# Moving the two x buffers from the end of each SBUF partition to the place ahead of the weights

## The chip, the cores and the metric

The kernel runs on one core of a Trainium2 chip. The metric is the device time of one execution in microseconds (us); three runs of the kernel before gave 540.85, 543.45 and 539.7, so the median is 540.85 us.

## What is computed

A linear-attention pass (4 sequences, 8 heads, 768 tokens, 48 channels per head) whose output feeds a gated feed-forward layer over 3,072 tokens. Its weights come as 64-bit floats, its other inputs as 32-bit floats. Cut to what matters:

```python
for t in range(S):                                   # attention, per batch and head
    cur = einsum('bhd,bhe->bhde', u[None] * k[:, :, t], v[:, :, t])
    y[:, :, t] = einsum('bhd,bhde->bhe', r[:, :, t], state + cur)
    state = w[None, :, :, None] * state + einsum('bhd,bhe->bhde', k[:, :, t], v[:, :, t])
x = y.transpose(0, 2, 1, 3).reshape(3072, 384)
gate = 1 / (1 + exp(-(x @ w_gate)))                   # 384 -> 1536
out = (gate * (x @ w_val)) @ w_out                    # 1536 -> 384
```

## The kernel before

Tokens go in 12 chunks of 64 per sequence. Two chunks of all four sequences make one tile `xt[ti]` of 512 token columns, so there are 6 tiles (`TILES`). The attention of a chunk runs in two groups of heads; each group's output is copied from PSUM into the tile's `xt` by ScalarE (`x_high`, L456, the part that the matmul format keeps) and VectorE (`x_low`, L460, the rest), and small DMAs of the SP queue (`fill`) put the rows of the last two heads into their places. Every tile lies in one of two buffers of 16,384 bytes in each of the 128 partitions, taken in turn.

The feed-forward layer takes a tile's 512 columns through 12 slices f of 128 hidden channels. `up(f)` (L502) issues 18 matmuls: for gate and value each, three slices kt of the 384 channels by three passes (low weights by high x, high by high, high by low), all 9 adding up in one PSUM bank of the ring of three. The moving operand (the one that streams through the array) is `xt[:, kt, b, cols]`, the stationary one a 128 by 128 block of `wx`. Every matmul is preceded by its own weight load. Then come sigmoid (L511, ScalarE), product (L515, VectorE), and the split of the result into `h` high (L520, ScalarE) and low (L524, GpSimd). `down(f)` (L540) issues 9 matmuls whose moving operand is `h` and whose stationary operand is the third part of the same `wx`, into three accumulators. It goes pass by pass over the three output parts; at f = 11 it goes part by part, three passes in a row into the same accumulator. In the last tile the third part is split into two halves of 256 columns, so that there `down` has 12 matmuls.

The order of the work is written out by hand: `START` for the first tile, where weights are also loaded and converted (columns there go in halves of 256 for f = 0 and 1), then the loop over the items of tiles 1 to 5, which sets the pieces of attention (lines L320, L348 and L403, matmuls of at most 64 columns) between `up` and the `down` of the slice before. `tc.manual_schedule` keeps that order on PE, SP, DVE, ACT and POOL; only places in memory and the waits are worked out by the program. So a `down(f-1)` stands on PE's queue right behind `up(f)` or behind a piece of attention.

Places come from the pools in the order in which they are opened. Behind the constants lie `wp` (12 weight buffers of 9,216 bytes), `hp` (`sg`), `hq` (`h`), `wtmp` (`wf`), `ach` (`chan`), `atk` (`toks`), `adk` (`dec`) and `xp` (`xt`). At the end, a conditional block recomputes everything in another way if a decay is out of range; with these inputs it isn't entered.

Of the kernel before, what the change touches and what calls it, by code (L numbers as in the profile page):

```python
# [9 lines left out]
F32 = mybir.dt.float32  # L10
F32R = mybir.dt.float32r
# [8 lines left out]
P = 128  # L20
# [4 lines left out]
CT = B * C  # L25
# [32 lines left out]
def rwkv_then_moe(ctx: ExitStack, tc: tile.TileContext, wd, ch, tk, rt, ut, wt, rk0, vn0, wd0, out):  # L58
    nc = tc.nc

    const = ctx.enter_context(tc.tile_pool(name="const", bufs=1))
    wp = ctx.enter_context(tc.tile_pool(name="wp", bufs=1))
    hp = ctx.enter_context(tc.tile_pool(name="hp", bufs=2))
    hq = ctx.enter_context(tc.tile_pool(name="hq", bufs=2))
# [4 lines left out]
    main = ctx.enter_context(ExitStack())  # L69
    ach = main.enter_context(tc.tile_pool(name="ach", bufs=3))  # L70
    atk = main.enter_context(tc.tile_pool(name="atk", bufs=3))
    adk = main.enter_context(tc.tile_pool(name="adk", bufs=2))
    xp = main.enter_context(tc.tile_pool(name="xp", bufs=2))


    def two_banks():
# [179 lines left out]
    xt, dec, ga, yb, kv = {}, {}, {}, {}, {}  # L256
# [180 lines left out]
    def x_of(n, k):  # L437
        c, g = GROUPS[n]
        ti = TILE_OF[c]
        if ti not in xt:  # L440

            xt[ti] = xp.tile([P, 4, 2, 512], F32R, name="xt")
        co = CT * TILES[ti].index(c)
        return [
            (
                xt[ti][lo:hi, 2 * g : 2 * g + 2, k, co + 128 * be : co + 128 * be + 128],
                yb[n][be][lo:hi, 0:256].rearrange("q (p x) -> q p x", p=2),
            )

            for be in range(2)  # L450
            for lo, hi in (((0, 48), (64, 112)) if ti == 0 and g == 0 else ((0, 112),))
        ]

    def x_high(n):
        for x, y in x_of(n, 0):
            nc.scalar.copy(out=x, in_=y)  # L456

    def x_low(n):
        for (x, y), (hi, _) in zip(x_of(n, 1), x_of(n, 0)):
            nc.vector.tensor_tensor(x, y, hi, ALU.subtract)  # L460
# [164 lines left out]
    for step in START.split():  # L625
        name, _, arg = step.partition(".")
# [22 lines left out]
    for i in range(n0, len(items)):  # L649
        ti, h, f = items[i]  # L650
# [44 lines left out]
    with tc.If(bad != 0):  # L695
        with ExitStack() as g:
            gp = g.enter_context(tc.tile_pool(name="gp", bufs=1))
# [21 lines left out]
            with tc.For_i(0, NC) as c:  # L719
# [38 lines left out]
                    out=xg[bass.ds(c, 1)].rearrange("o q p t -> (o q) p t"),  # L758
                    in_=yc.rearrange("q p b i -> q p (b i)"),
                )  # L760
            xr = gp.tile([P, 3, 2, CT], F32, name="xr")
            x = gp.tile([P, 3, 2, 512], F32R, name="xgr")
            with tc.For_i(0, NC, 2) as c:
                for j in range(3):
                    for to, lo, n, p in (
# [113 lines left out]
```

## Time and profile before

| what | value |
|---|---|
| median of three runs | 540.85 us (539.7 to 543.45) |
| profiled execution: first to last instruction | 538.6 us |
| what lies around that span, against the median | 540.85 - 538.6 = 2.25 us |
| mean granted TensorE clock | 0.996 |
| PE busy | 519.2 us, 96% of the span |
| DVE, ACT, POOL busy | 218.3, 171.8 and 175.0 us |

For the profiled execution the profile gives the span alone; its own time with what lies around it was not taken apart from the three runs. PE is TensorE's matmuls, PEld its weight loads, DVE the vector engine, ACT the scalar engine, POOL GpSimd. A matmul's duration runs from its issue to its modelled end, so it is longer than the step from one matmul to the next: steps are taken from the starts of a row of matmuls.

### The profile page before, as it was taken

How to read it: one execution, taken by the hardware profiler on the slowest of the kernel's cores; microseconds unless marked ns; L12 is line 12 of the kernel's file. 1: busy time of each engine (PE TensorE's matmuls, PEld its weight loads, DVE VectorE, ACT ScalarE, POOL GpSimd, SP SyncE). 2: the span in 40 equal slices, each digit the busy share in tenths (PEclk: the TensorE clock that was granted, in tenths of full speed). 3: DMA queues.
4: the chain of work that ended last, by engine and by line, in shares of the span. 5: the costliest groups of instructions: out<-in, count | busy, mean ns of one | idle time of the engine just before them, and what ended most of it. 6: DMA issues, size and time to landing. Idle time of an engine off the chain costs nothing.

```text
span 538.6 us, 12067 instructions
## 1 busy us (share of the span) xinstructions
PE 519.2 (96%) x5268; PEld 426.9 (79%) x5268; DVE 218.3 (41%) x379; ACT 171.8 (32%) x358; POOL 175.0 (32%) x156
## 2 busy tenths in 40 slices
PE   4879999999999999999999999999999999999996
PEld 3769878788788887888888888888888887888885
DVE  7798999942343342432423414313414311111111
ACT  5576654522132232231332222222322212221121
POOL 3353330002814444234145144144242311111120
PEclk9999999999999999999999999999999999999999
DMA  8886903053022213220303402203300001100001
GB/s 324 314 301 239 382 2 99 16 204 128 2 86 86 70 48 141 85 84 3 95 3 104 145 7 79 67 28 106 144 1 16 12 1 19 60 0 1 0 1 63
DMA packets 15707, 48.03 MB, mean 89 GB/s; under 512 B 2369, under 2 KB 5057, under 8 KB 14241
## 3 DMA queue, kind: packets, MB, share of 16 engines
q1 hardware_dynamic: 15360, 46.81, 25.2%
q8 instruction: 43, 0.70, 0.5%
q10 hardware_dynamic: 288, 0.39, 0.2%
q14 instruction: 16, 0.12, 0.1%
HBM read 40.12 MB, written 4.72 MB: 83 GB/s over the span
## 4 chain that ended last, share of the span: by engine, by line
PE 91%; DVE 4%; DMA 3%; ACT 1%; issue 0%; SPq 0%; DVEq 0%; ACTq 0%
PE ring L502 55%; PE acc L540 27%; PE ring L320 5%; PE sc L348 2%; DMA toks<-in_tk 1%; DMA chan<-in_ch 1%; PE sc L403 1%; DMA wr<-in_wt 1%; DVE score L362 1%; PE sc L540 1%; DVE wf L243 1%; DVE wf L244 1%; DVE wx L253 0%; ACT wf L236 0%; DVE wf L242 0%
## 5 line engine op out<-in xcount | busy, mean ns | idle before, releaser
L502 PE MATMUL ring<-xt,wx 128*128 128x512 f32 (+1 forms) x1332 | 317.1, 392 | 2.1 <-ACT wx L250 1.7
L502 PEld LDWEIGHTS ring<-xt,wx 128*128 128x128 f32 x1332 | 247.4, 191 | 57.5 <-ACT wx L250 1.9
L524 POOL TENSOR_TENSOR h<-sg,h 128x512 fp32r<-128x512 f32 (+1 forms) x68 | 91.8, 1350 | 332.4 <-ACT h L520 326.5
L540 PE MATMUL acc<-h,wx 128*128 128x512 f32 (+1 forms) x666 | 160.9, 383 | 0.0
L515 DVE TENSOR_TENSOR sg<-ring,sg 128x512 f32<-128x512 f32 (+1 forms) x74 | 50.0, 676 | 272.7 <-PE ring L502 272.7
L540 PEld LDWEIGHTS acc<-h,wx 128*128 128x128 f32 x666 | 119.6, 188 | 24.3
L511 ACT ACTIVATE sg<-ring 128x512 f32<-128x512 f32 (+1 forms) x74 | 43.4, 586 | 181.2 <-PE ring L502 181.2
L520 ACT CAST h<-sg 128x512 fp32r<-128x512 f32 (+1 forms) x74 | 45.3, 612 | 109.0 <-DVE sg L515 109.0
L422 ACT ACTIVATE state<-state,every 112x96 f32<-112x96 f32 x80 | 23.5, 363 | 26.7 <-PE ring L320 26.7
L460 DVE TENSOR_TENSOR xt<-ring,xt 112x256 fp32r<-112x256 f32 (+1 forms) x52 | 19.9, 418 | 26.9 <-ACT xt L456 26.9
L301 POOL TENSOR_TENSOR dec<-chan,every 128x512 f32<-128x512 f32 x20 | 23.8, 1190 | 13.8 <-PE ring L320 5.9
L362 DVE COPY_PREDICATED score<-masks,sc 128x512 f32<-128x512 int32 x32 | 23.8, 743 | 0.9
L456 ACT CAST xt<-ring 112x256 fp32r<-112x256 f32 (+1 forms) x52 | 17.1, 372 | 17.2 <-PE ring L320 15.6
L320 PE MATMUL ring<-score,toks 64*64 64x64 f32 (+1 forms) x768 | 18.6, 230 | 4.0 <-DVE score L362 2.0
L311 POOL TENSOR_TENSOR toks<-toks,tabn 128x384 f32<-128x384 f32 x18 | 19.7, 1093 | 0.0
L320 PEld LDWEIGHTS ring<-score,toks 64*48 64x48 f32 (+1 forms) x768 | 15.3, 133 | 5.2 <-POOL dec L301 1.9
L250 ACT CAST wx<-wf 128x1152 fp32r<-128x1152 f32 (+1 forms) x13 | 14.1, 1084 | 15.1 <-DVE wf L244 15.1
L244 DVE SCALAR_TENSOR_TENSOR wf<-wr,wf 128x1152 int32<-128x1152 int32 (+1 forms) x13 | 18.4, 1415 | 0.5
L320 PEld LDWEIGHTS ring<-dec,state 48*48 48x48 f32 (+1 forms) x704 | 12.0, 127 | 7.4 <-issue 6.7
L348 PE MATMUL sc<-dec,chan 48*64 48x64 f32 x768 | 17.6, 231 | 0.1
L289 POOL TENSOR_TENSOR dec<-dec,toks 128x384 f32<-128x384 f32 x16 | 16.3, 1016 | 1.2
L243 DVE SCALAR_TENSOR_TENSOR wf<-wr,wf 128x1152 int32<-128x1152 int32 (+1 forms) x13 | 16.5, 1266 | 0.5
(62 smaller groups left out, 253.0 us busy)
## 6 DMA issues: line engine op xcount, KB each, us to landing
wr<-in_wt SPq DMA_DIRECT2D x11, 1152.0 KB, 8.7
chan<-in_ch SPq DMA_DIRECT2D x24, 512.0 KB, 4.5
toks<-in_tk SPq DMA_DIRECT2D x24, 400.0 KB, 4.9
out_y<-wf SPq DMA_DIRECT2D x16, 256.0 KB, 2.3
dec<-in_rt SPq DMA_DIRECT2D x16, 192.0 KB, 2.6
xt<-xt SPq DMA_DIRECT2D x30, 64.0 KB, 2.3
wr<-in_wt SPq DMA_DIRECT2D x2, 576.0 KB, 5.2
xt<-xt SPq DMA_DIRECT2D x12, 32.0 KB, 4.9
```

What stands on the lines that cost most here:

```text
L244: nc.vector.scalar_tensor_tensor(g, low, 29, g, ALU.logical_shift_right, ALU.bitwise_or)
L301: eng.tensor_tensor(v4(t[:, 0]), v4(chan[n][:, 0]), bc2(table_of(n)), ALU.mult)
L320: nc.tensor.matmul(yb[n][bank][64 * half : 64 * half + m, cs], lhsT, rhs, start=first, stop=stop, skip_group_check=True,)
L348: nc.tensor.matmul(sc[64 * gm : 64 * gm + 64, be ^ gm, o : o + C], kk[row, cs : cs + C], rr[row, cs : cs + C], start=True, stop=True,)
L362: nc.vector.copy_predicated(t.rearrange("q (b m i) -> q b m i", b=2, m=4), masks[:, m].bitcast(I32).unsqueeze(1).unsqueeze(1).broadcast_to ...
L422: nc.scalar.activation(st[:, p, s], st[:, p, s], AF.Copy, scale=pw[0:112, 4 * g + 2 * p + s, 64:65],)
L502: nc.tensor.matmul(o[:, self.cols], w[a][:, g * DM + kt * P : g * DM + (kt + 1) * P], self.x[:, kt, b, self.cols], start=(k == 0), stop=(k ...
L511: nc.scalar.activation(sg[:, c], self.pair[f][0][:, c], AF.Sigmoid)
L515: nc.vector.tensor_tensor(sg[:, c], self.pair.pop(f)[1][:, c], sg[:, c], ALU.mult)
L520: nc.scalar.copy(out=h[:, 0, c], in_=sg[:, c])
L524: eng.tensor_tensor(h[:, 1, c], self.sg.pop(f)[:, c], h[:, 0, c], ALU.subtract)
L540: nc.tensor.matmul(acc[:, to], w[a][:, 2 * DM + d * P : 2 * DM + (d + 1) * P], h[:, b, cols], start=(f == 0 and k == 0 and self.cols.start ...
```

## The change

`xp` is opened right behind the constants, ahead of the weights, and stays open to the end; its tile gets the tag `xt`. The conditional block takes its two x tiles from `xp` under the same tag, since the room that they had lies elsewhere now.

```diff
     const = ctx.enter_context(tc.tile_pool(name="const", bufs=1))
+    xp = ctx.enter_context(tc.tile_pool(name="xp", bufs=2))
     wp = ctx.enter_context(tc.tile_pool(name="wp", bufs=1))
...
     adk = main.enter_context(tc.tile_pool(name="adk", bufs=2))
-    xp = main.enter_context(tc.tile_pool(name="xp", bufs=2))
...
-            xt[ti] = xp.tile([P, 4, 2, 512], F32R, name="xt")
+            xt[ti] = xp.tile([P, 4, 2, 512], F32R, name="xt", tag="xt")
...
-            xr = gp.tile([P, 3, 2, CT], F32, name="xr")
-            x = gp.tile([P, 3, 2, 512], F32R, name="xgr")
+            xr = xp.tile([P, 3, 2, CT], F32, name="xr", tag="xt")
+            x = xp.tile([P, 3, 2, 512], F32R, name="xgr", tag="xt")
```

In bytes from the end of the constants, worked out from the shapes of the tiles (r is the remainder of the offset by 512):

| tile | before | r | after | r |
|---|---|---|---|---|
| `xt`, two of 16,384 | 162,176 | 384 | 0 | 0 |
| `wx`, twelve of 9,216 | 0 | 0 | 32,768 | 0 |
| `sg`, two of 2,048 | 110,592 | 0 | 143,360 | 0 |
| `h`, two of 4,096 | 114,688 | 0 | 147,456 | 0 |
| `wf`, two of 4,608 | 122,880 | 0 | 155,648 | 0 |
| `chan`, three of 4,096 | 132,096 | 0 | 164,864 | 0 |
| `toks`, three of 3,200 | 144,384 | 0, 128, 256 | 177,152 | 0, 128, 256 |
| `dec`, two of 4,096 | 153,984 | 384 | 186,752 | 384 |

Both versions end at 194,944. A block that a weight load reads starts a multiple of 512 bytes into `wx`, and a 512-column slice of `xt` or `h` a multiple of 2,048 into its tile.

## Rows read from the trace of the kernel before

**Rows 1.** The page, part 1: busy time, share of the span, instructions.

```profile
PE 519.2 (96%) x5268; PEld 426.9 (79%) x5268; DVE 218.3 (41%) x379; ACT 171.8 (32%) x358; POOL 175.0 (32%) x156
```

**Rows 2.** The page, part 4: the chain that ended last, shares by line.

```profile
PE ring L502 55%; PE acc L540 27%; PE ring L320 5%; PE sc L348 2%; DMA toks<-in_tk 1%; DMA chan<-in_ch 1%; PE sc L403 1%; DMA wr<-in_wt 1%; DVE score L362 1%; PE sc L540 1%; DVE wf L243 1%; DVE wf L244 1%; DVE wx L253 0%; ACT wf L236 0%; DVE wf L242 0%
```

**Rows 3.** Stretches: length, busy us (count) per engine, granted clock, DMA share, GB/s.

```profile
57.77:83.03 25.26, 24.97 (x317) 20.32 (x316) 23.99 (x30) 14.52 (x24) 9.57 (x5) 1.00 0.34 139
83.03:466.50 383.47, 383.17 (x3577) 311.07 (x3576) 135.43 (x251) 106.31 (x222) 129.45 (x112) 1.00 0.22 68
466.50:538.60 72.10, 67.16 (x325) 55.81 (x323) 9.41 (x14) 13.76 (x23) 12.92 (x10) 0.99 0.03 12
```

**Rows 4.** Waits of PE's matmuls, 83 to 466 us: total us, times, longest.

```profile
PE ring L320 <- issue: 0.2, 1, 0.2
```

**Rows 5.** Groups by line and shape: busy us, mean ns | idle before.

```profile
L502 PE MATMUL ring<-xt,wx 128*128 128x512 f32 x1260 | 304.6, 395 | 0.0
...
L540 PE MATMUL acc<-h,wx 128*128 128x512 f32 x594 | 152.6, 395 | 0.0
...
L502 PE MATMUL ring<-xt,wx 128*128 128x256 f32 x72 | 12.5, 343 | 2.1 <-ACT wx L250 1.7 <-DVE wx L253 0.5
```

**Rows 6.** Timeline of PE from 460.1 us: start, length, work.

```profile
460.26 2.22 PE L540 MATMUL acc<-h,wx 128*128 128x512 f32 x9
462.31 4.36 PE L502 MATMUL ring<-xt,wx 128*128 128x512 f32 x18
466.50 0.74 PE L540 MATMUL acc<-h,wx 128*128 128x512 f32 x3
```

**Rows 7.** Groups of PE, 462.6 to 466.3 us.

```profile
L502 PE MATMUL ring<-xt,wx 128*128 128x512 f32 x18 | 4.4, 395 | 0.0
```

**Rows 8.** Timeline of PE, 101.05 to 103.6 us, within a double `down`.

```profile
100.70 3.11 PE L540 MATMUL acc<-h,wx 128*128 128x512 f32 x13
```

**Rows 9.** Groups of PE in the same stretch.

```profile
L540 PE MATMUL acc<-h,wx 128*128 128x512 f32 x13 | 3.1, 389 | 0.0
```

**Rows 10.** Timeline of PE, 48.8 to 50.0 us: `h` at 256 columns.

```profile
48.60 1.60 PE L540 MATMUL acc<-h,wx 128*128 128x256 f32 x12
```

**Rows 11.** Groups of PE in that stretch.

```profile
L540 PE MATMUL acc<-h,wx 128*128 128x256 f32 x12 | 1.6, 283 | 0.0
```

**Rows 12.** Timeline of PE, 31.4 to 32.9 us: x at 256 columns.

```profile
31.14 1.95 PE L502 MATMUL ring<-xt,wx 128*128 128x256 f32 x15
```

**Rows 13.** Groups of PE in that stretch.

```profile
L502 PE MATMUL ring<-xt,wx 128*128 128x256 f32 x15 | 1.9, 282 | 0.0
```

**Rows 14.** Timeline of all engines from 455.5 us.

```profile
455.70 1.30 POOL L524 TENSOR_TENSOR h<-sg,h 128x512 fp32r<-128x512 f32 x1 [5.38 <-ACT h L520]
...
461.78 0.58 ACT L554 COPY wf<-acc 128x512 f32<-128x512 f32 x1
...
461.95 1.30 POOL L524 TENSOR_TENSOR h<-sg,h 128x512 fp32r<-128x512 f32 x1 [4.95 <-ACT h L520]
```

**Rows 15.** The chain in order of time, last tile: start, us, what.

```profile
519.00 4.18 PE ring L502 x18
```

**Rows 16.** Groups by line and shape: writers of `xt` and of `wf`.

```profile
L460 DVE TENSOR_TENSOR xt<-ring,xt 112x256 fp32r<-112x256 f32 x44 | 16.6, 417 | 24.3 <-ACT xt L456 24.3
...
L456 ACT CAST xt<-ring 112x256 fp32r<-112x256 f32 x44 | 14.2, 373 | 16.5 <-PE ring L320 15.0 <-DVE state L433 1.5
...
L557 DVE COPY wf<-acc 128x256 f32<-128x256 f32 x5 | 2.1, 424 | 2.0 <-ACT wf L556 2.0
L556 ACT COPY wf<-acc 128x256 f32<-128x256 f32 x5 | 1.9, 373 | 0.8 <-PE acc L540 0.8
```

**Rows 17.** The page, part 6: DMA issues, KB each, us to landing.

```profile
xt<-xt SPq DMA_DIRECT2D x30, 64.0 KB, 2.3
```

**Rows 18.** Timeline, 292 to 304 us: a piece of attention.

```profile
299.89 0.68 PE L320 MATMUL ring<-dec,state 48*64 48x64 f32 x32
...
300.39 0.65 PE L348 MATMUL sc<-dec,chan 48*64 48x64 f32 x32
```

## The prediction

> **What bounds the kernel now.** I read the page's busy times first: PE is busy 96% of the span, no other engine over 41% [rows 1]. The chain of waits names the kind of PE work: 55% of the span is L502 (moving operand x), 27% L540 (moving operand h) [rows 2]. The stretches say where this holds: from 57.77 us on PE is busy all but 0.3 us of each stretch up to 466.5, at a granted clock of 1.00, the 2.4 GHz level [rows 3], and its matmuls wait 0.2 us in 383 [rows 4]. So from about 57 us to the end the time is the number of matmuls by the step from one to the next, and only what changes a step can change the time. No instruction, count or order changes here; places in memory alone do.
>
> So the question is whether the step depends on where an operand lies. The trace holds a comparison. Behind a run of x matmuls the next run of h starts at 466.50, the x run itself at 462.31 [rows 6]; 18 x matmuls last 4.36 us to the last end, one lasts 0.395 [rows 7], so a step is (4.36 - 0.395) / 17 = **233.2 ns**. In a long run of h, once it has settled, 13 last 3.11 and one lasts 0.389 [rows 8, 9]: (3.11 - 0.389) / 12 = **226.8 ns**. The two have the same 128 rows, 512 columns, format and clock, and a weight load ahead of each. There are 1,260 of the first kind and 594 of the second [rows 5].
>
> What else could tell them apart? An x run adds up 9 matmuls in one PSUM bank and uses the same weights twice in three steps, an h run changes bank and weights at each step. But at f = 11 `down` does both: three passes in a row into one accumulator, weights in the order of `up`. The run at 460.26 is such a one, since the copy of the accumulator into `wf` follows at 461.78 [rows 14]; it takes 462.31 - 460.26 = 2.05 us for 9 [rows 6], 227.8 a step with the first two still settling. Neither bank nor weight order slows it. What remains is the moving operand's tile. By the table of offsets x starts at remainder 384 by 512, and weights and h at 0; and x lies in the last 32,768 bytes that the program uses. Which of the two counts the trace can't say, as nothing else wide is read from there; the change alters both. After it x starts 114,688 + 32,768 = 147,456 bytes ahead of h, nine times 16,384, so every remainder by powers of two up to 16,384 is the same for x as for h.
>
> **The change part by part.**
>
> *L502 at 512 columns.* I let x take h's step: 233.2 - 226.8 = 6.4 ns. An `up` has 18: 0.115 us. There are 70 such `up`: 10 in tile 0, 48 in tiles 1 to 4, 12 in the last. The settling of h behind x goes too, 9 x (227.8 - 226.8) = 0.009 us. So 58 slices save 0.124 us each, 7.2 us. In the last tile an x run takes 4.18 on the chain [rows 15], 232.2 a step, so 18 x 5.4 = 0.097, by 12: 1.2 us; its `down` mixes 512 and 256 columns and I give it nothing. Sum **8.3 us**. The bounds: nothing at the one end, as no row shows an operand read from both places. At the other, the whole cost per matmul beyond its columns vanishes: h takes (1.60 - 0.283) / 11 = 119.7 ns at 256 columns [rows 10, 11], so 256 columns cost 107.1, 512 cost 214.2, and 1,260 x (233.2 - 214.2) = 23.9 us. The other sign is priced among the rivals. I take 8.3, since the nearest row is h, whose remainders x gets.
>
> Back-to-back weight loads and matmuls are the subject of the Trainium skill, TensorE: Matmul & The Clock Gate, Part 2 (Step-by-step: what each phase is for): PE has two independent read ports on SBUF, so that the next weights take no bandwidth from the running matmul. By that rule no place could collide with another, and the sum would be 0 us instead of 8.3; it is the first rival below.
>
> *L502 at 256 columns.* 72 of them [rows 5]. At 31.14 us 15 last 1.95 and one 0.282 [rows 12, 13], 119.1 a step, against h's 119.7. If x takes h's step it loses 72 x 0.6 = 0.04 us, and in that stretch PE waits for weights anyway: 0. This row also speaks against my reading: at 256 columns x pays nothing for its place. It says that the cost isn't one per matmul; a meeting of two streams at some point of the longer read would look so.
>
> *Writers of x.* ScalarE writes 112 x 256 to x in 373 ns and the same width to `wf`, which lies elsewhere, in 373; VectorE takes 417 and 424, though the first also reads x [rows 16]. Place costs them nothing: 0. If it did, PE covers it, as DVE and ACT are busy 135 and 106 of 383 us [rows 3].
>
> *DMAs.* The copies within x, 30 of 64 KB at 2.3 us [rows 17], keep partitions, sizes and their turn on SP's queue: 0; PE covers a slip as long as a tile's last fill lands before its first `up`. No step is moved past another on any queue, and no wait is added outside the conditional block.
>
> *Everything else* moves up by 32,768 bytes with its remainders unchanged: 0. Attention's operands get the place that x had; that is the slower rival.
>
> *Would a faster PE meet a wait?* The low half of h is ready at 455.70 + 1.30 = 457.00, and its `down` starts at 460.26 [rows 6, 14]: 3.3 us to spare, against 0.12 us that a slice loses. PE stays the bound, and the saving passes through.
>
> The sum is made on the profiled span: 538.6 - 8.3 = 530.3. The median of the runs stands 2.25 above that span, so 540.85 - 8.3 = **532.5 us**.
>
> **The rivals.**
>
> *Place is nothing (same).* The 6.4 ns belong to something of L502 that stays, such as the ring's banks or the length of its runs. For it: at 256 columns there is no difference [rows 10 to 13]. Against it: the f = 11 run shares its order and its bank use with x and steps at 227.8 [rows 6]. Time: 540.85 us. The rule of the two ports gives the same 540.85; the trace doesn't bear it out so far, as its two kinds of steps differ by 6.4 ns in spite of equal sizes, but it shows no collision as such either. I put half of this rival's chance on it.
>
> *Part of it.* The remainder matters, but x's step and h's lock in only some runs, as the unsettled first steps behind each change of line suggest. Half the gain, 4.2 us, is 536.7, within 1%.
>
> *The end of the partition costs, and attention inherits it (slower).* If what lies in the last 32,768 bytes is read more slowly by PE, x leaves and `dec` with parts of `chan` and `toks` arrive. The page counts 5,268 matmuls [rows 1]; `up` has 1,332, `down` 74 x 9 + 12 x 3 = 702, so about 3,200 small ones are left. If each paid 6.4 ns in full, that is 20.5, and less the 8.3 the kernel would take 553 us. It decides from (8.3 + 5.4) / 3,200 = 4.3 ns each, which makes it 1% slower. Against it: 32 of them start in 300.39 - 299.89 = 0.50 us, 15.6 ns apart [rows 18], several in the array at once, so that a price per matmul would be shared (by four: 5.1 us, a net gain of 3); and x's 256-column reads from that place paid nothing.
>
> *It doesn't do what it says.* The places are worked out from shapes; if the pools were laid out in another order, x would keep its place: 540.85, part of the first rival.
>
> **How the numbers follow.** Forecast (x takes h's step, gain 6 to 10 us, 531 to 535): 0.62. More, towards 214 ns a step: 0.04. Place is nothing: 0.18, on half of it the rule. Part: 0.08. Slower: 0.08. A measurement of this kernel tells about 1% (5.4 us) from no change. So faster by over 1%: 0.66, within: 0.26, slower: 0.08. The range reaches from 530, just under the forecast's own 531 to 535, over the part and the unchanged case to 541.5; it leaves out the slower case, the large gain, and the upper part of the spread of unchanged runs, some 0.17 in all.
>
> **What would show it.** Right: L502's 18 matmuls start-to-start in 18 x 226.8 = 4.08 us instead of 4.19, single ones at 389 ns instead of 395, `down` settled from its first steps, PE still busy 383 of 383 us before the last tile. Wrong: L502 at 233 (place is nothing), attention's 32 in over 0.55 us (the end costs), or a new idle time of PE before L540.

## The result, and the profile after

The changed kernel takes 534.18 us (median of 4 runs, 532.61 to 536.21) against 540.75 for the kernel before on the same chip: ratio 0.9868, 95% interval 0.9833 to 0.9903. In a later comparison it took 533.32 against 541.12, ratio 0.9855 (0.9838 to 0.9873). The forecast was 532.5, within 530.0 to 541.5.

The costliest groups of the kernel after, by line and shape (busy us, mean ns | idle before), answer to [rows 5]:

```profile
L502 PE MATMUL ring<-xt,wx 128*128 128x512 f32 x1260 | 297.2, 389 | 0.0
...
L540 PE MATMUL acc<-h,wx 128*128 128x512 f32 x594 | 152.1, 394 | 0.0
```

A matmul of x now takes the 389 ns that a settled one of h took before [rows 9]; before it took 395. The timeline of PE in the kernel after, at the same place in the program as [rows 6]:

```profile
452.62 2.20 PE L540 MATMUL acc<-h,wx 128*128 128x512 f32 x9
454.67 4.24 PE L502 MATMUL ring<-xt,wx 128*128 128x512 f32 x18
458.75 0.73 PE L540 MATMUL acc<-h,wx 128*128 128x512 f32 x3
```

From the start of the 18 matmuls of x to the next line are 458.75 - 454.67 = 4.08 us, where it was 4.19; a step is (4.24 - 0.389) / 17 = 226.5 ns, where it was 233.2.

PE is the bound as before, as the stretches of the kernel after show (length, busy us per engine, granted clock, DMA share, GB/s; they begin and end at the same places of the program as [rows 3], to within 0.2 us):

```profile
57.00:81.81 24.81, 24.52 (x316) 20.13 (x315) 23.45 (x30) 14.37 (x23) 9.18 (x5) 1.00 0.28 117
81.81:458.70 376.89, 376.59 (x3577) 311.10 (x3576) 135.13 (x251) 106.26 (x222) 128.97 (x112) 1.00 0.22 69
458.70:530.80 72.10, 66.24 (x325) 55.68 (x324) 9.41 (x14) 13.77 (x23) 12.93 (x10) 0.98 0.04 12
```

The same 3,577 matmuls of the middle stretch take 376.59 us instead of 383.17, with the same count and nearly the same busy time on every other engine.

The span went from 538.6 to 530.8, 7.8 us, but not all of that is the change's. Its part lies between the first `up` of 512 columns and the end of the last matmul, where PE hardly waits. From the starts in the traces, in us from the start of the span (the last three rows are runs described below):

| run | first `up` of 512 columns | first `up` of the last tile | end of the last matmul | first to end | span |
|---|---|---|---|---|---|
| before | 50.28 | 456.06 | 533.66 | 483.4 | 538.6 |
| after | 49.43 | 448.54 | 524.94 | 475.5 | 530.8 |
| after, second execution | 50.81 | 449.92 | 526.32 | 475.5 | 531.3 |
| x at the end, remainder 0 | 49.68 | 448.77 | 525.17 | 475.5 | 531.7 |
| x in front, remainder 384 | 50.28 | 456.04 | 533.63 | 483.4 | 538.9 |

So the change is worth 7.9 us, the same in both profiled executions of it: 6.7 up to the last tile and 1.2 in it. What comes ahead of the first `up` of 512 columns differs by 1.4 us between these two, what comes behind the last matmul by 0.9, and the span with them. The clock differs too. In the kernel before, the granted clock had fallen to the lower of its two levels, 1.2 GHz, for a part of the stretch from 38 to 48 us, after PE had waited 1.68 us for weights:

```profile
39.02 6.20 PE L502 MATMUL ring<-xt,wx 128*128 128x256 f32 x36 [1.68 <-ACT wx L250]
...
38.00:48.00 10.00, 8.80 (x196) 8.36 (x196) 8.09 (x14) 5.55 (x13) 4.73 (x4) 0.83 0.61 216
```

In the profiled execution of the kernel after, with waits of 0.34 and 1.28 us there, it had not:

```profile
37.85 0.47 PE L502 MATMUL ring<-xt,wx 128*128 128x256 f32 x2 [0.34 <-DMA xt<-xt]
39.60 4.34 PE L502 MATMUL ring<-xt,wx 128*128 128x256 f32 x34 [1.28 <-DVE xt L460]
...
38.00:48.00 10.00, 8.43 (x203) 7.75 (x204) 9.60 (x18) 6.44 (x16) 5.76 (x4) 1.00 0.67 232
```

In the second profile of the changed kernel it had fallen too (0.83), behind a wait of 2.48 us. So this comes and goes with the execution, not with the place of x.

### The profile page after: what moved, and what is told of

Same layout as the page of the kernel before. It is cut to its first block, busy times and chain, and to the rows that moved or that the text cites. A ratio compares the mean times of both kernels' runs of the same rounds, so it can differ in the third digit from the quotient of the medians.

```text
span 530.8 us, 12067 instructions
## 1 busy us (share of the span) xinstructions
PE 510.1 (96%) x5268; PEld 425.4 (80%) x5268; DVE 217.8 (41%) x379; ACT 172.0 (32%) x358; POOL 174.2 (33%) x156
## 4 chain that ended last, share of the span: by engine, by line
PE 92%; DMA 3%; DVE 3%; issue 1%; SPq 0%; ACT 0%; DVEq 0%
PE ring L502 55%; PE acc L540 28%; PE ring L320 5%; PE sc L348 2%; DMA toks<-in_tk 1%; DMA chan<-in_ch 1%; PE sc L403 1%; DMA wr<-in_wt 1%; PE sc L540 1%; DVE score L362 1%; DVE xt L460 0%; DVE wf L243 0%; DVE wx L253 0%; DVE wf L242 0%; DVE sg L515 0%
## 5 line engine op out<-in xcount | busy, mean ns | idle before, releaser
L502 PE MATMUL ring<-xt,wx 128*128 128x512 f32 (+1 forms) x1332 | 308.2, 385 | 2.1 <-DVE xt L460 1.3
L502 PEld LDWEIGHTS ring<-xt,wx 128*128 128x128 f32 x1332 | 245.8, 189 | 51.1 <-DVE xt L460 1.5
L540 PE MATMUL acc<-h,wx 128*128 128x512 f32 (+1 forms) x666 | 160.3, 382 | 0.0
L540 PEld LDWEIGHTS acc<-h,wx 128*128 128x128 f32 x666 | 119.5, 188 | 23.4
L287 POOL TENSOR_TENSOR dec<-dec,ub 128x384 f32<-128x384 f32 x16 | 16.7, 1046 | 0.0
```

The costliest lines, as they stand in the source:

```text
L502: nc.tensor.matmul(o[:, self.cols], w[a][:, g * DM + kt * P : g * DM + (kt + 1) * P], self.x[:, kt, b, self.cols], start=(k == 0), stop=(k ...
L540: nc.tensor.matmul(acc[:, to], w[a][:, 2 * DM + d * P : 2 * DM + (d + 1) * P], h[:, b, cols], start=(f == 0 and k == 0 and self.cols.start ...
```

## The experiments

The question left open was what it is about the place: the end of the partition (theory E), the remainder of x's address against the weights' (R), or the remainder of x's own address (A). The line numbers of `up` (L502) and `down` (L540) shift by one or two where an edit adds or removes lines. In the experiments that need room, the two helper masks `later` and `same` lie in the score tiles, which are cleared afterwards anyway:

```diff
-    later = const.tile([P, P], F32, name="later")
-    same = const.tile([P, P], F32, name="same")
+    later, same = score[0][:, 0:P], score[1][:, 0:P]
```

**x at the end, at remainder 0.** From the kernel before, with the masks moved and a gap ahead of x:

```diff
+    gap = main.enter_context(tc.tile_pool(name="gap", bufs=1))
     xp = main.enter_context(tc.tile_pool(name="xp", bufs=2))
...
+    gap.tile([P, 160], F32, name="gap")
```

> The kernel before with x still behind everything else, but at remainder 0 by 512 from the weights instead of 384 (the two helper masks share the room of the score tiles, which frees 1,024 bytes; a gap of 640 stands ahead of x). Theory R (the remainder of x against the weights counts): L502 steps at 226.7 ns, the time is that of the changed kernel, 534 us. Theory E (the end of the partition counts): L502 stays at 233 ns, 540.8 us. Theory A (the remainder of x's own address counts, whatever the weights): as R, 534 us.

Measured: 532.83 us against 541.58, ratio 0.9842 (0.981 to 0.9873). Groups of PE:

```profile
L503 PE MATMUL ring<-xt,wx 128*128 128x512 f32 x1260 | 297.2, 389 | 0.0
L541 PE MATMUL acc<-h,wx 128*128 128x512 f32 x594 | 152.1, 394 | 0.0
```

To the tenth of a microsecond these are the numbers of the kernel after, with x still the last tile of the partition. E is refuted.

**x in front, at remainder 384.** From the kernel after, with the masks moved and 128 bytes between x and the weights:

```diff
+    gap = ctx.enter_context(tc.tile_pool(name="gap", bufs=1))
     wp = ctx.enter_context(tc.tile_pool(name="wp", bufs=1))
...
+    gap.tile([P, 32], F32, name="gap")
```

> The changed kernel with a gap of 128 bytes between x and the weights: x stays in front, but at remainder 384 by 512 from the weights; h and the weights keep remainder 0 to each other. R: L502 at 233 ns, L540 settles at 226.7, 540.8 us. E: L502 at 226.7, 534 us. A: x's own address keeps its remainder, so L502 at 226.7, 534 us.

Measured: 540.9 us against 541.58, ratio 0.9995 (0.9977 to 1.0013). Groups of PE:

```profile
L503 PE MATMUL ring<-xt,wx 128*128 128x512 f32 x1260 | 304.6, 395 | 0.0
L541 PE MATMUL acc<-h,wx 128*128 128x512 f32 x594 | 152.6, 394 | 0.0
```

128 bytes give the whole gain back: 304.6 and 395 are the numbers of [rows 5]. x's own address has the remainder that it has in the fast version, so A falls too; and the weights moved together with h, whose settled steps are still 226 and 227 ns, so it isn't the weights' own alignment either. What counts is the difference of the two. R stands.

**A sweep of the remainder.** From the kernel after, with the masks moved and every weight buffer 64 bytes longer:

```diff
-            wparts[f] = wp.tile([P, 2, W3], F32R, name="wx", tag=f"w{f}")
-            whi[f], wlo[f] = wparts[f][:, 0], wparts[f][:, 1]
+            wparts[f] = wp.tile([P, 2 * W3 + 16], F32R, name="wx", tag=f"w{f}")
+            whi[f], wlo[f] = wparts[f][:, 0:W3], wparts[f][:, W3 : 2 * W3]
```

> The changed kernel with each of the 12 weight buffers 64 bytes longer, so that slice f's weights stand at remainder 64 f by 512 from x, and h at 256 from x. R: L502's step depends on f and repeats after 8 slices: 226.7 ns at f = 0 and 8, 233 at f = 2 and 10 (the 384 of the kernel before); L540 has its 226.7 at f = 4. The other remainders show how fine the effect is; a step under 226.7 at one of them would be a better place. E and A: the same step, 226.7, at every f.

The expectation put slice f's buffer at the f-th place. That was wrong: the buffers lie in the order of their first use, slices 11, 0, 1, 2, 4, 7, 3, 5, 6, 10, 9, 8, so slice 0 stands at 64, slice 1 at 128, slice 2 at 192 and slices 11, 4 and 6 at 0 by 256. The timeline of PE, the runs of x in slices 0 to 6 of the fifth tile in turn (start, length):

```profile
373.08 4.36 PE L501 MATMUL ring<-xt,wx 128*128 128x512 f32 x18
379.34 4.36 PE L501 MATMUL ring<-xt,wx 128*128 128x512 f32 x18
...
387.83 4.28 PE L501 MATMUL ring<-xt,wx 128*128 128x512 f32 x18
394.04 4.35 PE L501 MATMUL ring<-xt,wx 128*128 128x512 f32 x18
400.29 4.24 PE L501 MATMUL ring<-xt,wx 128*128 128x512 f32 x18
...
408.66 4.29 PE L501 MATMUL ring<-xt,wx 128*128 128x512 f32 x18
414.84 4.24 PE L501 MATMUL ring<-xt,wx 128*128 128x512 f32 x18
```

4.24 us is the fast kernel's length, 4.36 the slow one's: slices 4 and 6, at remainder 0 by 256, have the one, slices 0, 1 and 3 at 64, 128 and 128 the other, slices 2 and 5 at 192 lie between. Slices 11, 4 and 6 stand at 0, 256 and 0 by 512, and all three are at the floor. h stands 256 bytes off x here and follows the same pattern with the same slices (the last four steps of its runs take 227 to 229 ns on the mean at 0, 233.4 at 64, 233 to 234 at 128, 229 to 230 at 192). So the period is 256, not the 512 of the prediction's table.

**Finer remainders.** The same, with the weights placed within their longer buffers:

```diff
+PLACE = (11, 0, 1, 2, 4, 7, 3, 5, 6, 10, 9, 8)
+SHIFT = (8, 32, 32, 48, 16, 0, 16, 32, 32, 16, 48, 56)
...
+            o = SHIFT[PLACE.index(f)] // 4
-            whi[f], wlo[f] = wparts[f][:, 0:W3], wparts[f][:, W3 : 2 * W3]
+            whi[f], wlo[f] = wparts[f][:, o : o + W3], wparts[f][:, o + W3 : o + 2 * W3]
```

> The sweep again with finer remainders. The weight buffers lie in the order of their first use (11, 0, 1, 2, 4, 7, 3, 5, 6, 10, 9, 8), and read in that order the sweep before has a period of 256 bytes: 226.7 ns at 0, 233.3 at 64, 232.5 at 128, 228.9 at 192. Here the weights' remainder by 256, less that of x, is 8, 96, 160, 240, 16, 64, 144, 224, 32, 80, 176 and 248 in that order. R as a meeting of two streams: a smooth or stepped curve between those four values, with 226.7 the floor, in L502 and L540 alike. R as alignment alone: anything but 0 is slow, 8 and 248 too. If some remainder gives a step under 226.7, there is a better place than that of the changed kernel. Theory B (the weights' own alignment to some block, whatever the moving operand) can't be told from R here, as x and h have the same remainder.

The step of `up` at 512 columns, worked out from the starts in the two traces as the mean from the eighth step of each run on, by the weights' remainder by 256 less that of x:

| remainder | 0 | 8 | 16 | 32 | 64 | 80 | 96 | 128 | 144 | 160 | 176 | 192 | 224 | 240 | 248 |
|---|---|---|---|---|---|---|---|---|---|---|---|---|---|---|---|
| ns | 226.7 | 230.7 | 227.8 | 233.3 | 233.3 | 232.0 | 234.1 | 232.7 | 233.5 | 233.5 | 230.3 | 228.8 | 233.4 | 227.3 | 233.3 |

Of the 15, only 0 and its neighbours at 16 bytes to either side are near the floor; at 8 bytes off it is partly or wholly lost, so this is neither a smooth curve nor an alignment to 0 alone. The means at 16 and 240 hide two kinds of runs: each stands for one slice in six tiles, and at 16 five of its runs step at 226.7 and the one in the last tile at 233.3, at 240 four at 226.7 and two at 228.5. So 16 bytes off can cost nothing, but isn't safe; at 0 all 18 runs are at the floor. Nothing is under 226.7. The times of the two sweeps, 540.93 and 540.31 us in one run each, mix fast and slow slices and carry no verdict.

**The two halves of the weights apart.** From the kernel after, with the masks moved; at every other place in memory the low half stands 128 bytes further from the high half, so that the pairs (high, low) go through (0,128), (128,128), (128,0), (0,0):

```diff
+            o = 32 if PLACE.index(f) % 2 == 0 else 0
-            wparts[f] = wp.tile([P, 2, W3], F32R, name="wx", tag=f"w{f}")
-            whi[f], wlo[f] = wparts[f][:, 0], wparts[f][:, 1]
+            wparts[f] = wp.tile([P, 2 * W3 + o], F32R, name="wx", tag=f"w{f}")
+            whi[f], wlo[f] = wparts[f][:, 0:W3], wparts[f][:, W3 + o : 2 * W3 + o]
```

> The changed kernel with the low half of the weights apart from the high half: by place in memory, the remainders (high, low) by 256 against x are (0,128), (128,128), (128,0), (0,0), and so on in fours. A run takes its weights as low, high, high. N (what is read while x streams are the next matmul's weights, so the next one's remainder counts): with (0,128) the slow steps are those whose next weights are low, one in three, with (128,0) the two others. O (a matmul's own weights count): with (0,128) the slow steps follow a low matmul. Both: (0,0) steps at 226.7, (128,128) at 232.5 to 233.3, (0,128) a third and (128,0) two thirds of the way, unless steps take several matmuls to settle, as they do behind a change of line.

Steps in ns, from the starts in the trace, of one run each; the first step goes from a low to a high matmul, the second from high to high, the third from high to low, and so on:

```
(0,0)    227 226 227 227 226 227 227 226 227
(0,128)  234 227 232 234 227 233 234 226 233
(128,0)  231 233 232 235 233 232 235 233 232
```

The timeline of PE around the first two (slice 6 at (0,128), then slice 8 at (0,0), with slice 7 at (128,128) between them):

```profile
413.66 4.32 PE L503 MATMUL ring<-xt,wx 128*128 128x512 f32 x18
...
419.86 4.35 PE L503 MATMUL ring<-xt,wx 128*128 128x512 f32 x18
...
427.97 4.25 PE L503 MATMUL ring<-xt,wx 128*128 128x512 f32 x18
```

Neither N nor O holds alone. With only the low half off, both steps next to a low matmul are slow, the one into it and the one out of it, and the step between two high ones is at the floor: two in three are slow, not one. With the high half off all three are. In these patterns a step is at its floor only if the weights in use and those that come next both have the right remainder. The single run took 539.04 us.

**dec aligned too.** From the kernel after:

```diff
-    atk = main.enter_context(tc.tile_pool(name="atk", bufs=3))
     adk = main.enter_context(tc.tile_pool(name="adk", bufs=2))
+    atk = main.enter_context(tc.tile_pool(name="atk", bufs=3))
```

> The changed kernel with the pools of dec and toks exchanged, so that dec goes from remainder 384 to 0 (toks keep 0, 128 and 256). R, if it holds for attention's small matmuls too: the pieces of 32 matmuls of dec by chan and dec by state (0.50 us start to start) get shorter by up to 3%, 0.015 us by some 60 pieces, 1 us at most: 533 to 534. If it counts only for long reads of 512 columns: the time of the changed kernel, 534, and pieces of 0.50 us.

Measured: 532.18 us against 541.58, ratio 0.9847 (0.981 to 0.9883), an interval that overlaps that of the changed kernel. A piece of attention in the timeline of PE:

```profile
295.71 0.68 PE L320 MATMUL ring<-dec,state 48*64 48x64 f32 x32
296.21 0.65 PE L348 MATMUL sc<-dec,chan 48*64 48x64 f32 x32
296.68 0.58 PE L403 MATMUL sc<-toks 64*48 64x48 f32 x30
```

and the same one in the kernel after:

```profile
294.97 0.68 PE L320 MATMUL ring<-dec,state 48*64 48x64 f32 x32
295.47 0.65 PE L348 MATMUL sc<-dec,chan 48*64 48x64 f32 x32
295.93 0.58 PE L403 MATMUL sc<-toks 64*48 64x48 f32 x30
```

The 32 take 0.50 us from their start to that of the next line in both, as in [rows 18]. Attention's small matmuls show no effect of this shift of dec, the only one tried, and their operands' move to the end of the partition cost nothing.

**Only three pools in another order, beside the changed kernel.** From the kernel before:

```diff
-    atk = main.enter_context(tc.tile_pool(name="atk", bufs=3))
     adk = main.enter_context(tc.tile_pool(name="adk", bufs=2))
     xp = main.enter_context(tc.tile_pool(name="xp", bufs=2))
+    atk = main.enter_context(tc.tile_pool(name="atk", bufs=3))
```

> The kernel before with nothing but the order of three pools changed, dec, x, toks in place of toks, dec, x. x stays in the last third of the partition, 9,600 bytes lower, and its remainder from the weights is 0 by 512 since the three token tiles of 3,200 bytes no longer stand ahead of it. R: L502 at 226.7 ns, time as the changed kernel run beside it, 533 to 534. E, or something of L502 that stays: 233 ns, 540 to 541.

> The changed kernel once more, beside the one with toks last. R: both the same within 0.5%, 533 to 534. If place in front is worth something of its own beside the remainder, this one is faster than the other by more than that.

Measured: 533.79 us, ratio 0.9867 (0.9842 to 0.9893), with toks last; 533.32, ratio 0.9855 (0.9838 to 0.9873), for the changed kernel; both spans are 531.3. With toks last the timeline of PE has, at the place of [rows 6],

```profile
456.02 4.24 PE L502 MATMUL ring<-xt,wx 128*128 128x512 f32 x18
460.10 0.73 PE L540 MATMUL acc<-h,wx 128*128 128x512 f32 x3
```

4.08 us from start to start, as in the kernel after. Place in front is worth nothing beside the remainder, as far as the measurement tells. No version tried is faster than the changed kernel beyond the measurement.

## Why the prediction was right

- *PE's step is the bound, and x's step depends on its place:* right. The start-to-start of 18 matmuls was forecast to fall from 4.19 to 4.08 us and did; the single matmul from 395 to 389 ns and did.
- *Which property of the place:* left open between remainder and end; the change altered both, so the forecast did not have to choose. The end is refuted by x at the end and fast, the remainder shown by x in front and slow. The table of remainders goes by 512; the sweep gives a period of 256.
- *The sum:* 8.3 us on the span, though its own terms, 7.2 and 1.2, make 8.4; measured 7.9. The term that was too large is that of the 58 slices up to the last tile: 6.7 of 7.2. By the starts in the traces, x's steps there gave 6.4 of the 6.7 that 58 x 18 x 6.4 ns makes: from step to step within a run they fell by 6.2 ns on the mean (233.25 to 227.02), since some first steps are still unsettled. The settling of h gave 0.3 of 0.5. Behind x's runs `down` is settled from the start, as forecast, 0.015 us less in each of 37; but behind a piece of attention it settles more slowly than before, 2.34 us instead of 2.32, and 17 runs give 0.015 us each back. In the last tile the 1.2 came, partly by luck: 0.9 from x, and 0.3 from `down`, to which the forecast gave nothing. The medians gained 6.6 us in the first comparison and 7.8 in the second.
- *256 columns, writers, DMAs, other tiles:* nothing, as forecast. x's first 18 matmuls of 256 columns at the full clock take 2.42 us in the kernel after, 2.41 before. The row at 256 columns, which spoke against the reading, was no counter-evidence: in the last 18 such matmuls the steps go between 112 and 123 ns before and are all 120 after, so the remainder shows there too, but it lengthens the mean only at the longer read.
- *No new wait:* right. In the middle stretch PE's matmuls wait 0.2 us, as in [rows 4], and the low half of h is ready at 454.32 + 1.29 = 455.61, 3.1 us ahead of the `down` at 458.75:

```profile
PE ring L320 <- issue: 0.2, 1, 0.2
...
454.32 1.29 POOL L524 TENSOR_TENSOR h<-sg,h 128x512 fp32r<-128x512 f32 x1 [4.83 <-ACT h L520]
```

- *The rivals:* "place is nothing" fell, and with it what the prediction drew from the rule of the two ports. The Trainium skill, TensorE: Matmul & The Clock Gate, Part 2 (Step-by-step: what each phase is for), has the next weights load through a port of their own without taking bandwidth from the running matmul. Here a shift of 128 bytes between the two operands (x in front, at remainder 384 instead of 0), with the same instructions in the same order, is worth 6.6 ns in 226.7 at each settled matmul of 512 columns; the measurement decides: with ports of their own, the step still depends on where the two lie. "The end costs and attention inherits it" fell with the unchanged 0.50 us.

What stays open is the cause behind the remainder. The runs show that the step depends on the difference of addresses by 256 bytes, of the weights in use and of those that follow; they do not show what waits for what, nor why some runs at 16 bytes off are at the floor and others not.

## What to carry to other kernels

When PE is the bound and every matmul has its own weight load, compare the steps of matmuls of equal shape whose moving operands lie in different tiles; a difference of a few ns with no wait in the profile can be an address. For matmuls like these (32-bit operands, 128 by 128 weights, 512 columns) keep the weights' blocks and the moving tile at the same remainder by 256 bytes: here a tile of 3,200 bytes (12.5 times 256) ahead of x, three times over, had put it 128 off and cost about 1.4% of the kernel. Pools whose sizes aren't multiples of 256 go last. Other formats and widths than those shown here were not tried.

## What was not expected of the hardware

- The penalty is not smooth in the remainder: 32 bytes off costs 6.6 ns a step, 8 bytes 4.0 to 6.6, and 16 bytes nothing in nine runs of twelve, 1.8 in two and 6.6 in one.
- A matmul's step depends on the remainders of two sets of weights, its own and the next: with the low half alone 128 bytes off, 234, 227 and 232 to 233 ns in turn.
- Where the remainder is wrong, the steps follow patterns of their own: 229 and 238 ns in turn, or a longer turn with one of 241. Several matmuls pass until the steps settle after a change of tile or width; where the remainder is right, there are only steps of 226 and 227 once they have settled.
